# One fused attention and MLP kernel: the written order of its 1,553 jobs and 83 engine choices replaced by others

## The chip, the cores and the metric

The kernel runs on one core of a Trainium2 chip. The metric is the device time of one launch in microseconds (us). The engines are TensorE (PE in the profile, with PEld for the loading of weights), VectorE (DVE), ScalarE (ACT) and GpSimd (POOL). SyncE (SP) issues nearly all DMAs. Each engine works through a list of its own in the order in which it is written, and waits at an instruction whose input is not there yet.

## What is computed

The attention output goes into a gated MLP with a product over the sequence, and this into a second MLP with a short convolution and a sigmoid gate. Everything is float32.

```python
# attention: batch 2, 8 heads, seq 768, head_dim 64
k_sum = max of k over blocks of 32;  v_sum = mean of v over blocks of 32
scores = [band |i-j| < 16 of scale * q k^T,  scale * q k_sum^T + log(32)]
attn   = softmax(scores) @ [v, v_sum]
# first MLP: d_model 512, d_ff 1024
h = relu(x @ w_in); u, v = halves of h; v_n = layer norm of v
v_s = w_spatial @ v_n (over seq) + b_spatial
y = (u * v_s) @ w_out
# second MLP: conv over seq with 3 taps
h = relu(y @ w_in2); gate = sigmoid(conv(h)); out = (h * gate) @ w_out2
```

## The kernel before

All large products are made of three matmuls (mm3, L320 to L322): operands are split in a high part (cast, L295) and a low part (subtract, L289), and hi*hi, lo*hi and hi*lo are summed in PSUM. A product of 512 columns is three matmuls in a row, and the low part of an operand is the last that such a product waits for.

**The front** is attention, interleaved with the first product of the first MLP (x @ w_in). The 16 groups i = 0 to 15 are eight pairs of heads n, two halves g each. One group is a chain over the engines: qk on PE (L472, L479, L485), row maximum on DVE (L489), six exps on ACT (L493), their total and its reciprocal on DVE (L496, L499), the normalisation on POOL or DVE (L502), two times three transposes on PE into the PSUM tile pt (L506), each followed by a copy into SBUF on ACT or DVE (L528), and the product with the values on PE (pv, L512). Its output is copied on ACT or DVE (L533) and its low part subtracted on DVE (L534). Two score buffers (s_80 and s_81 in the lists of order below) and one pt bank are shared by all groups, so that the next qk or transpose needs the reader of the one before to be done.

Two side jobs stand in the front. The **block means** of v are made on PE from the window tile `vwin` for the pairs n = 0 and 2 (L428), and for the others on DVE with a transpose on PE (L435, L438), and are spread by L440 and L447. The **conversion of w_in** to a high and a low part takes a multiply on ACT or POOL (L304, L305), a shift (L307) and two operations on DVE that read two SBUF operands each (L309, L311), a cast and a subtract. L400, L408 and L414 prepare the windows of k and their maxima.

**The middle** is dense: the rest of the first product, the product over the sequence, the merge of w_out with w_in2 and the product with it, all mm3. **The last layer** works on halves of both operands (L716 makes sums of blocks, L295 and L289 split them, L874 mixes finished PSUM tiles into outputs) and stores the output.

**What sets the order.** A Plan collects all 1,553 jobs with what each depends on. Two tables then rule: ORDER holds the job numbers as pairs of base-64 signs, and the jobs are written to the program in this order; PICK holds, for each job that can run on more than one engine, which one is taken. So each engine's list, and the list of the DMAs that SP issues, is cut out of one order written by hand. Where the plan's own costs leave PE a gap of 0.5 us or more in the front, it writes in matmuls on `ones` (L932) that nobody reads: 17 of them in the kernel before, 6 ahead of the first qk, then 1, 8 and 2 ahead of the later ones.

Of the kernel before, what the change touches and what calls it, by code (L numbers as in the profile page):

```python
# [20 lines left out]
B, H, S, D = 2, 8, 768, 64  # L21
# [1056 lines left out]
```

## Time and profile before

| | us |
|---|---|
| median of 3 runs (330.38 to 330.89) | 330.82 |
| the profiled execution's own time | 332.48 |
| its span, first to last instruction | 330.7 |
| PE busy | 320.4 (97%) |
| DVE busy | 270.9 (82%) |
| ACT busy | 206.5 (62%) |
| POOL busy | 109.3 (33%) |

PE is the busiest by far. What it does not do in the span, about ten microseconds, lies at the start, in the first 80 us, in a short place of the last layer, and behind the last matmul. From 81 us to 284 us PE has no idle time that the table of stretches shows. The granted clock of TensorE is 1.00 in every stretch.

### The profile page before, as it was taken

The page shows a single profiled execution, that of the slowest core. Times are in us where ns is not written, and L with a number is a line of the kernel's source. Part 1 is how long each engine was busy: PE and PEld are TensorE (multiplying, and loading weights), DVE is VectorE, ACT ScalarE, POOL GpSimd, SP SyncE. Part 2 cuts the span into 40 slices and gives each one's busy share as a digit, 9 for nine tenths or more (in the row PEclk, how much of TensorE's full clock was granted, in tenths as well). Part 3 has the DMA queues.
Part 4 walks back from the last instruction along what each step waited for, and adds up shares of the span by engine and source line. Part 5 has one row for each costly group of instructions (what it writes and reads, how often), then busy time and mean ns, then how long its engine had stood idle before and what let it go on. Part 6 is the DMA issues. An engine that isn't in the chain of part 4 may idle for free.

```text
span 330.7 us, 6432 instructions
## 1 busy us (share of the span) xinstructions
PE 320.4 (97%) x2414; PEld 272.0 (82%) x2414; DVE 270.9 (82%) x501; ACT 206.5 (62%) x516; POOL 109.3 (33%) x129
## 2 busy tenths in 40 slices
PE   8887999999999999999999999999999999999995
PEld 3566878868888888888888888888888899999894
DVE  5996988997677517888969989899979999988882
ACT  3887988867456354625335545779978898955410
POOL 4686776543252146003101313020301320345510
PEclk9999999999999999999999999999999999999999
DMA  7968794842011540341333423350511330255234
GB/s 236 321 210 236 238 288 157 273 135 72 2 63 51 192 140 34 107 133 66 126 92 116 152 87 127 127 97 1 96 25 22 52 68 2 43 126 119 50 113 152
DMA packets 16640, 39.25 MB, mean 119 GB/s; under 512 B 2016, under 2 KB 8160, under 8 KB 16608
## 3 DMA queue, kind: packets, MB, share of 16 engines
q1 hardware_dynamic: 13728, 34.11, 31.6%
q0 software_dynamic: 2880, 4.72, 8.1%
q8 instruction: 19, 0.31, 0.4%
q14 instruction: 13, 0.11, 0.1%
HBM read 30.96 MB, written 3.15 MB: 103 GB/s over the span
## 4 chain that ended last, share of the span: by engine, by line
PE 85%; DVE 9%; DMA 2%; ACT 2%; issue 1%; DVEq 0%
PE late L320 11%; PE late L321 11%; PE late L322 11%; PE mm L320 8%; PE mm L321 8%; PE mm L322 8%; PE xp L321 3%; PE pt L506 3%; PE pt L321 3%; PE xp L322 3%; PE pt L320 3%; PE pt L322 3%; PE xp L320 3%; PE xp L512 3%; DMA a<-vwin 2%; DVE a L311 2%
## 5 line engine op out<-in xcount | busy, mean ns | idle before, releaser
L493 ACT ACTIVATE a<-s,a 128x120 f32<-128x120 f32 x96 | 33.2, 375 | 2.1 <-DVE a L489 2.1
L289 POOL TENSOR_TENSOR w<-a,w 128x256 fp32r<-128x256 f32 (+1 forms) x14 | 14.8, 1058 | 38.5 <-ACT w L295 38.2
L322 PE MATMUL late<-xh,a 128*128 128x512 f32 (+1 forms) x72 | 26.7, 371 | 0.0
L321 PE MATMUL late<-xl,a 128*128 128x512 f32 (+1 forms) x72 | 26.7, 371 | 0.0
L320 PE MATMUL late<-xh,a 128*128 128x512 f32 (+1 forms) x72 | 26.7, 371 | 0.0
L502 POOL TENSOR_TENSOR a<-a,a 128x720 f32<-128x720 f32 x15 | 21.3, 1422 | 9.5 <-DVE a L499 7.5
L295 ACT CAST xh<-tmp 128x384 fp32r<-128x384 f32 (+2 forms) x32 | 15.8, 510 | 9.1 <-DVE tmp L716 5.6
L752 DVE SCALAR_TENSOR_TENSOR w<-v,conv_t,w 128x1534 f32<-128x1534 f32 x10 | 18.2, 1816 | 4.0 <-ACT w L748 3.8
L493 ACT ACTIVATION_READ_ACCUMULATOR a<-s,a 128x1 f32 x96 | 21.3, 222 | 0.0
L311 DVE SCALAR_TENSOR_TENSOR a<-a,a 128x512 uint32<-128x512 uint32 (+1 forms) x24 | 18.6, 776 | 0.6
L506 PE MATMUL pt<-ident,a 128*120 128x128 f32 x96 | 16.4, 280 | 2.1 <-DVE a L528 1.8
L289 DVE TENSOR_TENSOR xl<-tmp,xh 128x384 fp32r<-128x384 f32 (+2 forms) x31 | 17.9, 586 | 0.1
L528 ACT COPY a<-pt 120x384 f32<-120x384 f32 x24 | 11.6, 482 | 9.5 <-PE pt L506 9.3
L575 DVE BATCH_NORM_STATS2 stat<-tmp 128x6 f32<-128x512 f32 x12 | 8.3, 691 | 11.2 <-ACT tmp L572 11.1
L304 ACT ACTIVATE a<-a 128x512 f32<-128x512 f32 (+1 forms) x16 | 10.1, 629 | 11.4 <-POOL w L289 4.5
L309 DVE SCALAR_TENSOR_TENSOR a<-a,a 128x512 uint32<-128x512 uint32 (+1 forms) x24 | 16.0, 665 | 1.4 <-ACT a L304 0.8
L489 DVE TENSOR_REDUCE a<-s 128x6 f32<-128x720 f32 x16 | 14.2, 890 | 3.4 <-PE s L485 3.4
L295 ACT CAST w<-a 128x512 fp32r<-128x512 f32 (+1 forms) x16 | 9.1, 566 | 12.3 <-DVE a L311 12.1
L506 PEld LDWEIGHTS pt<-ident,a 128*120 128x120 f32 x96 | 10.7, 137 | 7.0 <-DVE a L528 2.5
L320 PE MATMUL mm<-xh,a 128*128 128x512 f32 (+1 forms) x44 | 16.0, 364 | 0.0
L322 PE MATMUL mm<-xh,a 128*128 128x512 f32 (+1 forms) x44 | 16.0, 364 | 0.0
L321 PE MATMUL mm<-xl,a 128*128 128x512 f32 (+1 forms) x44 | 16.0, 364 | 0.0
(350 smaller groups left out, 1117.6 us busy)
## 6 DMA issues: line engine op xcount, KB each, us to landing
a<-w_in SPq DMA_DIRECT2D x12, 512.0 KB, 3.7
a<-w_out SPq DMA_DIRECT2D x8, 512.0 KB, 3.6
a<-vwin SPq DMA_DIRECT2D x8, 288.0 KB, 6.8
a<-v_in SPq DMA_DIRECT2D x6, 384.0 KB, 5.7
a<-vwin SPq DMA_DIRECT2D x4, 576.0 KB, 5.7
tmp<-w_spT SPq DMA_DIRECT2D x6, 384.0 KB, 3.1
a<-w_in SPq DMA_DIRECT2D x8, 256.0 KB, 6.2
a<-w_outT SPq DMA_DIRECT2D x4, 512.0 KB, 3.7
```

Source lines behind the costliest of these rows:

```text
L289: eng.tensor_tensor(out=lo.r(), in0=src.f(), in1=hi.f(), op=ALU.subtract)
L295: us = {"ACT": (0.2 + n / 1200, lambda: ACT.copy(hi.r(), src.f())), "POOL": (0.12 + n / 1050, lambda: POOL.tensor_copy(hi.r(), src.f()))}
L309: add({"DVE": (0.16 + n / 960, lambda: DVE.scalar_tensor_tensor(out=last.u(), in0=fu.u(), scalar=0x80000000, in1=last.u(), op0=ALU.bitwise ...
L311: add({"DVE": (0.16 + n / 960, lambda: DVE.scalar_tensor_tensor(out=fu.u(), in0=fu.u(), scalar=3, in1=last.u(), op0=ALU.logical_shift_left ...
L320: PE.matmul(ps, lhsT=lh, rhs=rh, start=first and i == 0, stop=False, **kinds)
L321: PE.matmul(ps, lhsT=lh, rhs=rl, start=False, stop=False, **kinds)
L322: PE.matmul(ps, lhsT=ll, rhs=rh, start=False, stop=last and i == n - 1, **kinds)
L489: DVE.tensor_reduce(out=st[:, 0], in_=sv, op=ALU.max, axis=AX.X, negate=True)
L493: ACT.activation(out=e[:, u, :NK], in_=sv[:, u // GA, u % GA], func=AF.Exp, bias=st[:, 0, u:u + 1], accum_out=sm[:, u, :1])
L502: eng.tensor_tensor(out=e, in0=e, in1=st[:, 1].unsqueeze(2).to_broadcast([128, GB, NK]), op=ALU.mult)
L506: PE.transpose(pt3[:NK, a], e[:, GA * h + a, :NK], ident)
L752: DVE.scalar_tensor_tensor(out=two(ct)[:, bs, to], in0=two(h)[:, bs, of], scalar=scale(k), in1=two(ct)[:, bs, to], op0=ALU.mult, op1=ALU.add)
```

## The change

Nothing but the two tables is replaced. The same jobs are written in another order, and some run on another engine. The first 481 places of the new ORDER hold the attention front and the first part of the first product; the later jobs stand in another order as well. Of the choices in PICK 83 differ. Over the program POOL has 12 rows fewer and DVE 2 more. In the part up to the small conversion of the convolution's weights (L974) DVE has three L528 copies more, one L502, one L400 and one L414 more, two L447 and one L440 less. The matmuls on `ones` go from 17 to 15: 6 ahead of the first qk, 5 ahead of the second, 4 ahead of the transposes of group 2.

```diff
--- before.py
+++ after.py
 ORDER = (
-    "ABASACAFAEAUAGAiATADAHAjAgAkAAAhALAqAVAWAIAMBKBYAXArAYA3BaAZAsANAJBbBZBL
...
+    "AAACABADAFAgAEAiAGAjAZAaAkAhAbAHAqAcAdAeArALBYAfAMBZBbBaBcAIA3A4AsAJAlAt
...
 )
 PICK = (
...
-    "111111010100101001011100110000000010000101001100010010000001110000001200
...
+    "001101210000101011001110100010000010100011000100011010100010111010000100
...
```

**First place, DVE.** This is DVE's list around the row maximum of group 2 (L489 on s_80) in the kernel before, up to the first copy of transposes (L528). a_0_124 and a_0_195 are the buffers in which w_in is converted.

```order
L489 TENSOR_REDUCE a_0_90<-s_80 128x6
L496 TENSOR_REDUCE a_0_95<-a_0_95 128x6
L499 RECIPROCAL a_0_95<-a_0_95 128x6
L309 SCALAR_TENSOR_TENSOR a_0_97<-a_0_124,a_0_97 128x256
L311 SCALAR_TENSOR_TENSOR a_0_195<-a_0_195,a_0_97 128x256
L408 TENSOR_REDUCE a_0_90<-a_0_91 128x12
L528 COPY a_0_92<-pt 120x384
```

The same place after the change, where a_0_156 is the buffer of the conversion:

```order
L307 TENSOR_SCALAR a_0_97<-a_0_156 128x256
L309 SCALAR_TENSOR_TENSOR a_0_97<-a_0_156,a_0_97 128x256
L311 SCALAR_TENSOR_TENSOR a_0_156<-a_0_156,a_0_97 128x256
L499 RECIPROCAL a_0_90<-a_0_90 128x6
L489 TENSOR_REDUCE a_0_90<-s_80 128x6
L496 TENSOR_REDUCE a_0_95<-a_0_95 128x6
L499 RECIPROCAL a_0_95<-a_0_95 128x6
L408 TENSOR_REDUCE a_0_90<-a_0_91 128x12 x2
L528 COPY a_0_92<-pt 120x384
```

The conversion in the second buffer (a_0_195) has left this place. One conversion, L307, L309 and L311 of 256 columns, stands ahead of the row maximum, and between the row maximum and the copy L528 stand only two short operations and the two L408.

**Second place, PE.** This is PE's list around the block means of pair n = 2 (mm_85 is the PSUM tile of the means, L428). Before, the first half stands behind the transposes of group 5, with the scores of group 7 behind it:

```order
L485 MATMUL s_80<-a_0_95,a_0_231 64x120 x12
L438 MATMUL xp<-ident,a_0_86 24x128
L506 MATMUL pt<-ident,a_0_100 120x128 x3
L428 MATMUL mm_85<-a_0_233,a_0_86 24x128 x6
L472 LDWEIGHTS ones
L472 MATMUL s_81<-a_0_86,ones 64x3x24
```

After the change:

```order
L485 MATMUL s_81<-a_0_95,a_0_252 64x120 x12
L512 MATMUL xp<-a_0_92,a_0_492 64x64 x12
L506 MATMUL pt<-ident,a_0_91 120x128 x3
L428 MATMUL mm_85<-a_0_236,a_0_86 24x128 x12
L506 MATMUL pt<-ident,a_0_91 120x128 x3
L512 MATMUL xp<-a_0_92,a_0_492 64x64 x12
```

Both halves of the means now stand together, behind the scores of group 7, a product L512 of group 4 and the first transposes of group 6; ahead of that there is also one product of the first MLP of 256 columns.

**Third place, DVE in the last layer.** Before, between the mixes L874 of the second output half, w_1_2380 being the last of two, and the next mix:

```order
L874 TENSOR_TENSOR w_1_2380<-mm_85,w_1_2380 128x384
L716 TENSOR_TENSOR a_2_2617<-tmp_0_1227,w_1_2533 128x384
L289 TENSOR_TENSOR xl_0_102<-tmp_0_1227,xh_0_101 128x384
L716 TENSOR_TENSOR tmp_0_1227<-tmp_0_1227,w_1_2696 128x384
L289 TENSOR_TENSOR xl_0_102<-a_2_2617,xh_0_101 128x384
L716 TENSOR_TENSOR tmp_0_1227<-tmp_0_1227,w_1_2607 128x384
L289 TENSOR_TENSOR xl_0_104<-tmp_0_1227,xh_0_103 128x384
L289 TENSOR_TENSOR xl_0_102<-tmp_0_1227,xh_0_101 128x384
L874 TENSOR_TENSOR w_1_2533<-w_1_2533,late_1299 128x384
```

After the change:

```order
L874 TENSOR_TENSOR w_1_2412<-mm_85,w_1_2412 128x384
L716 TENSOR_TENSOR a_2_2663<-tmp_0_1208,w_1_2526 128x384
L289 TENSOR_TENSOR xl_0_102<-tmp_0_1208,xh_0_101 128x384
L716 TENSOR_TENSOR tmp_0_1208<-tmp_0_1208,w_1_2572 128x384
L289 TENSOR_TENSOR xl_0_102<-a_2_2663,xh_0_101 128x384
L289 TENSOR_TENSOR xl_0_102<-tmp_0_1208,xh_0_101 128x384
L874 TENSOR_TENSOR w_1_2464<-pt,v_2_2846 128x384
```

Two operations fewer stand between the mixes and the last subtract into xl: one sum L716 and one subtract L289 are elsewhere. POOL's list has three L289 in a row here, into xl_0_102, xl_0_104 and xl_0_99, where before it had an L289 into xl_0_104, a sum L716 and an L289 into xl_0_99.

## Rows read from the trace of the kernel before

**Rows 1.** the page: time of each engine, then shares of the chain that ended last

```profile
PE 320.4 (97%) x2414; PEld 272.0 (82%) x2414; DVE 270.9 (82%) x501; ACT 206.5 (62%) x516; POOL 109.3 (33%) x129
...
PE 85%; DVE 9%; DMA 2%; ACT 2%; issue 1%; DVEq 0%
```

**Rows 2.** busy us by stretch (x matmuls or operations), PEclk, DMA share, GB/s

```profile
0.00:21.00 21.00, 18.24 (x240) 10.72 (x242) 16.17 (x50) 13.73 (x56) 13.11 (x27) 1.00 0.81 261
21.00:41.00 20.00, 18.00 (x351) 13.99 (x346) 16.71 (x38) 16.97 (x79) 14.27 (x19) 1.00 0.80 232
41.00:61.00 20.00, 19.71 (x261) 16.63 (x264) 17.37 (x37) 17.79 (x63) 12.42 (x16) 1.00 0.74 234
61.00:81.00 20.00, 19.28 (x246) 15.64 (x236) 18.59 (x31) 13.74 (x55) 9.35 (x9) 1.00 0.45 139
...
284.00:315.00 31.00, 30.56 (x176) 29.89 (x175) 27.09 (x53) 18.86 (x46) 15.89 (x17) 1.00 0.39 84
```

**Rows 3.** waits view of PE: line, awaited engine, tile and line: us, times, longest

```profile
PE mm L428 <- DMA a<-vwin: 1.9, 2, 1.7
PE pt L506 <- DVE a L528: 1.8, 2, 1.2
PE mm L932 <- DVE mhalf L926: 1.0, 1, 1.0
PE xp L321 <- DVE xl L289: 0.4, 1, 0.4
```

**Rows 4.** timeline of DVE, 11 to 17 us: start us, us, line, tiles

```profile
11.66 1.54 DVE L309 SCALAR_TENSOR_TENSOR a<-a,a 128x256 uint32<-128x256 uint32 x1
...
14.23 0.38 DVE L309 SCALAR_TENSOR_TENSOR a<-a,a 128x256 uint32<-128x256 uint32 x1
14.53 1.61 DVE L311 SCALAR_TENSOR_TENSOR a<-a,a 128x256 uint32<-128x256 uint32 x1
```

**Rows 5.** timeline of POOL in the same stretch

```profile
14.46 1.40 POOL L502 TENSOR_TENSOR a<-a,a 128x720 f32<-128x720 f32 x1 [1.54 <-DVE a L499]
```

**Rows 6.** timeline of PE, 12 to 22 us; in brackets idle time before it

```profile
12.57 1.49 PE L428 MATMUL mm<-a,a 96*24 96x128 f32 x12 [0.16 <-DMA a<-vwin]
...
17.12 0.54 PE L506 MATMUL pt<-ident,a 128*120 128x128 f32 x3 [1.16 <-DVE a L528]
...
21.53 0.52 PE L506 MATMUL pt<-ident,a 128*120 128x128 f32 x3 [0.27 <-POOL a L414]
```

**Rows 7.** timeline of SP's issue and of PE's means, 21 to 28 us

```profile
21.29 2.84 SPq L386 DMA_DIRECT2D a<-vwin  x3
...
27.92 0.94 PE L428 MATMUL mm<-a,a 96*24 96x128 f32 x7 [1.73 <-DMA a<-vwin]
```

**Rows 8.** timeline of POOL, DVE and PE, 67 to 71 us

```profile
67.56 1.83 POOL L502 TENSOR_TENSOR a<-a,a 128x720 f32<-128x720 f32 x1
...
68.18 1.77 DVE L311 SCALAR_TENSOR_TENSOR a<-a,a 128x512 uint32<-128x512 uint32 x1
...
70.47 0.54 PE L506 MATMUL pt<-ident,a 128*120 128x128 f32 x3 [0.61 <-DVE a L528]
```

**Rows 9.** groups by line on DVE, 5 to 105 us: count, busy us, mean ns

```profile
L528 DVE COPY a<-pt 120x384 f32<-120x384 f32 x8 | 4.4, 548 | 1.6 <-PE pt L506 1.6
...
L447 DVE TENSOR_SCALAR a<-a 24x768 f32<-24x768 f32 x2 | 1.2, 615 | 0.2 <-ACT a L440 0.2
...
L502 DVE TENSOR_TENSOR a<-a,a 128x720 f32<-128x720 f32 x1 | 0.9, 899 | 0.0
```

**Rows 10.** timeline of POOL, DVE and PE in the last layer, 308 to 314 us

```profile
310.30 1.33 POOL L289 TENSOR_TENSOR xl<-tmp,xh 128x384 fp32r<-128x384 f32 x1
...
308.91 0.55 DVE L289 TENSOR_TENSOR xl<-tmp,xh 128x384 fp32r<-128x384 f32 x1
309.38 1.38 DVE L716 TENSOR_TENSOR tmp<-tmp,w 128x384 f32<-128x384 f32 x1
...
313.85 0.45 PE L321 MATMUL xp<-xl,a 128*128 128x384 f32 x1 [0.44 <-DVE xl L289]
```

More of the change, by code (lines that the diff above doesn't have):

```diff
@@ new lines @@
+    "CuClCmCnEfCKC3CvCwCaDhDMBPDWBQFNE0DiCxEpCyCzDXC0DYEqErDsCBDxDNDODPBWDjFMDZDaDAC5DtDQFOFPDkDlC6DbDcE1E2DmDnCCDyEUFVDdDoEs"
+    "EtDpEuC7C8C9C+C-BXEiDqDBCLFiEvFjE3E4EjEkDzD0EwFvCMCNDuDvCOCPD6DCDDDED7D8D9D1D+D2EEEFD3FBCQEGE5EmDFDGFkEHEIE6D4F6F7EOEPEQ"
+    "ERGmD5F8F9C4FCD-EAEBECFWEXE7FFFGEYEZEaEbGnFHFIFJFKElFXEDE8GlEcEdE9FYFLGkFZFlFaGQGRGDE+ExEJEKELESHRGSGEGFEyFmE-FAFnEzFbFz"
+    "F0EMFwGtG6GdEVJ8FQFRFcFdF1ENHHHIGeF2F3GfGGGgF4FeHSFSFTF5FoHJFUHTGhGiGjFpFqFrGuFDG7HUHVHKHLEWFsG8GTGUGHF+GVGIFtHMHNFuFfFg"
@@ new lines @@
+    "HlHmFxHnHoGJFyG9G+HOHWHbHcGvGKGwHdHXFhHpHYItGLGMF-GxGyGAHZH5GBHqIDH6HeGWGXIyGCH7FEGoH8HPHfHgGYHrHvGNGZGaGbHwHxHaGOGcGPHh"
+    "G-J5GzJ6GpG0HQH9H+HyGqLNIEG1G2GsGrH-IFIuHAHzH0HBIzINIOIPHCIIIvHsIAHiH1H2HtHuHDH3H4IBICIXIiI0HEG3IJIKHFLOLPHGILISI1G4G5Hj"
+    "I2HkITInIdIaIUIQIYIZIMLQIjIqIVIWIkIlIGIRIoIpI6LRIHIbIcI3JHJIJJImIrIeJbLbI9I+JKIwJvI7IsJ7LUI8IfIxIgI4I5JLJMJNJwI-JAJBJCKH"
+    "JDIhJcJRKbKIJSJxKcKdJTJlJEJUJdJOKJLWJmJyJVKRJ9JnKlKeJFJ+J-KKKLJeKMKSJWKmJGJzKAKfJPJ0JQJfJXJoJ1LDJ2J3KvKwJYJZJpK5KBJgLSJ4"
@@ new lines @@
+    "JaKNJhKCJiJqK6JjJrKOLELFK7LTLGLVMrJsKDKxLXMsMhKPJtLYKELZKnKgKFKTJkLaLdLcMiKUJuLiLeLfKhLgLpKoKiKpLhKjMjLkKyK8KqKGKVM-LjKW"
+    "KzLlK9MkLmLrLnKkLwKrMlLoLqK0NAMtKXKsMmKQLsLtM1KYK1LuK+MnK-LvLHLxM2MuKtK2LyLzK3L3KZL0LANTL1K4L+L2M3MvNJM4MoKaLIL4NdL5MwNK"
+    "M5MpL6L7KuLJL8L9MxM6NeNBL-M7NCMFMyMAMBMCNUMDMzNfMqLKMEM0NDNLNnNVLBNgOvNhMGNiNoM8LLMHOpMMNMMINEOqMTNWNXMJLCNYM9MKNZO1NFML"
+    "OrNjO2MOO3NkMNMPMQNpO4MVOsNqOwMaNNMRLMNOMSNrOxMUNlNxM+OtNsPHNaMWMXO7MYNGOuO8OyMZO9NPNtPTNmNQO5MbMcN4MdOzMeNRNHNyMfPUPVNz"
@@ L78 @@
+    "TrVyTuWdTbUAV7VrWhVzTtVPWBVsWnWwWVUHTkVtV0VUXVWxWeVVV1UBVSWiTnV2VuV3ToXdWyXZWpVXVQVvWfVwXeUIWqWoWLW0TpTvVWXaWzWFXfWMWNW7"
+    "W1TwWjXGXbWsVxW3VYWrUQWuWkW8WGW2WHWOXHWIWvV8WCW9XcWPWtXIXTXRWJW+WQW4XJXgW5XCW-X-X5V4XDXmXhXNUCXnXiXOW6XoXjXpXKXkXqXlXAXM"
+    "XBV9XEWKYAXLXyXzXrX0X6WDXPXFT8XsXQX1XtXSX7V+WEXUYBXXX2XWX3XuXvYCX8XwX4XxYLXYYDYFYGYMX9YNYEYOYHYPYIX+YJYQYK"
 )
 PICK = (
[L80 removed]
@@ L84 @@
+    "011000000000000100000000000000000000000000000000000000000000000000000000000000000000000000100010000000000000100000001000"
+    "0000001001000100000000001010100"
 )
```

43 lines of the change are left out of this document (13 added, 30 removed).

## The prediction

> **What bounds the kernel now.** The first view to read is the page's time by engine and its chain: PE is busy for 320.4 us of the 330.7 us of the span, and 85% of the chain that ended last is PE [rows 1]. Both tables of the change only move work that already exists, so the question is where PE stands still, and the table of busy time by stretch tells that [rows 2]. PE stands idle for 21.00 - 18.24 = 2.76 us in the first 21 us, 2.00 us from 21 to 41, 0.29 us from 41 to 61, 0.72 us from 61 to 81, and 0.44 us from 284 to 315. The stretches between have none. These five make 6.21 us; the rest lies behind the last matmul, where mixes and stores follow that no order of the earlier jobs shortens. The waits view names what PE waits for [rows 3]: 1.9 us on DMAs of vwin ahead of the block means, 1.8 us on DVE's copies out of pt, 1.0 us at the very start on a constant, which every order has, and 0.4 us on a subtract in the last layer. So at most 6.21 - 1.0 = 5.2 us of idle time can be won, the 1.0 being that of the start.
>
> Two timelines show why DVE is late. In the first, L309 and L311 of 256 columns, which read two SBUF operands, take 1.54 and 1.61 us, where the same L309 takes 0.38 us a moment later [rows 4]. POOL's L502 runs from 14.46 to 15.86 in the same time [rows 5], and L311 ends 0.3 us behind it. The copy L528 stands behind L311 on DVE, and so PE's transposes at 17.12 come after 1.16 us of waiting [rows 6]. At 68 us the pattern repeats: POOL's L502 from 67.56 to 69.39, L311 stretched to 1.77 us, and PE waits 0.61 us [rows 8]. In the last layer a sum L716 takes 1.38 us beside POOL's L289, where a subtract of the same size takes 0.55 us, and PE waits 0.44 us [rows 10].
>
> **The change part by part.** I take five terms: three stretches of the front, the last layer, and what the new order may cost unseen.
>
> A, the first 21 us. The new order has the same attention work on PE up to the transposes of group 2, and the same nine matmuls on `ones` behind the first qk (5 and 4 in place of 1 and 8). What goes is the wait of 1.16 us: the second conversion leaves its place ahead of the copy, and what is left between the row maximum and the copy are reductions. The 0.27 us at 21.53 [rows 6] goes too. Of the idle 2.76 us, 1.0 stays, so 1.7 us can be won at most, and nothing if new waits come for old. New waits are likely here: the first block means now stand ahead of the third qk, and their vwin, though issued some places earlier, is among the first DMAs; before, the means waited 0.16 us for it at 12.57 [rows 6]. The DMA engines are at 0.81 of their time [rows 2], so some other load pays for each that is moved up. I take half of the gain, -0.9 us, with -1.7 and 0 as bounds.
>
> B, 21 to 41 us. The largest single wait of PE is here: vwin of pair 2 is issued at 21.29, and the means start at 27.92 after 1.73 us [rows 7]. Now the first half of the means stands behind a product of 256 columns, the scores of group 7, a product L512 and transposes of group 6. The transposes alone take 0.54 us [rows 6]; I estimate the four jobs at four times that, some 2 us, which is more than the wait. And the issue itself, which waits for the product L512 of group 0 to release the buffer, comes as much earlier as PE gains in A. So the first half should find its data. The second half now follows at once, while its vwin can be issued only when the product of group 1 has released its half of the buffer; it takes part of the wait over. I take half, -0.9 us of the 2.00 idle, with -1.8 and 0 as bounds.
>
> C, 41 to 105 us. The idle time is 0.29 + 0.72 = 1.01 us. Its main row, 0.61 us at 70.47 [rows 8], goes with a collision that the new lists avoid as far as they show it: the L502 of POOL that met the conversion of 512 columns stands among reductions and copies of DVE. I take -1.0 us; 0 is the other bound.
>
> D, the last layer. Between the mixes and the last subtract DVE has five operations in place of seven. Each is worth 0.47 us, the step from one start at 308.91 to the next at 309.38 [rows 10], so DVE reaches the subtract that PE awaits about 0.9 us earlier, and the 0.44 us can go: -0.4 us. POOL's three L289 in a row of 1.33 us each [rows 10] are on the other side. Each can hold a DVE operation for 1.38 - 0.55 = 0.83 us, and two more such meetings than before would cost up to 1.7 us. Bounds -0.4 and +1.7.
>
> E, what an order does not show. The three meetings of [rows 4, 8, 10] cost PE 1.16 + 0.61 + 0.44 = 2.2 us. An order does not say which of two operations starts first, and others will meet; so I charge a fifth of that, +0.4 us, bounds 0 and +1.5.
>
> Of these meetings the rows show that an operation of DVE with two SBUF operands takes 1.54 us where it takes 0.38 us by itself [rows 4]. The Trainium skill ("SBUF — State Buffer", section "Who interferes with whom") states that DVE's second read port is shared with GpSimd, that the first to start holds it for its whole operation, and that DVE operations with at most one SBUF input outside its two-port modes do not contend. By that rule an order that lays reductions beside POOL's operations pays nothing, E would be 0 and the sum -3.2 us, 327.6 us; the trace agrees in so far as the stretched rows all have two SBUF operands, and the rule speaks against the last layer, below.
>
> The work itself is nearly level: of L528, L502 and L447, DVE gets 3 x 0.55 + 0.90 - 2 x 0.615 = 1.3 us more [rows 9], hidden as long as DVE has gaps: 40 - 17.37 - 18.59 = 4.0 us from 41 to 81 [rows 2].
>
> The sum is -0.9 - 0.9 - 1.0 - 0.4 + 0.4 = **-2.8 us**. The profiled execution took 332.48 us, 1.8 us more than its span of 330.7, so a profile of the changed kernel should show a span near 327.9. The median of 330.82 is 1.66 us under that execution; I subtract the same 2.8 us from it, which gives 328.0 us.
>
> **The rivals.** *DVE becomes the bound (slower).* Place: 41 to 81 us, where DVE has 4.0 us of gaps [rows 2]. It gets 1.3 us more from the three groups above, and if four of its two-operand operations there meet POOL that do not now, at 1.38 - 0.55 = 0.83 us each [rows 10], 3.3 us more: 4.6 us. It decides from the point at which the gaps cannot take that in; row maxima must follow their scores at once, so I count half of the gaps as usable, and 2.6 us are left over. Then C does not come, and A and B come half: 330.8 + 2.6 - 0.9 = 332.5 us. For it speaks the density, DVE being busy for 18.59 of 20 us from 61 to 81; against it, that the new list has fewer conversions directly ahead of copies.
>
> *The front is bound by loads.* DMA engines are busy 0.81 and 0.80 of the first 41 us [rows 2], and each wait on a copy is only followed by one on q or vwin. Then A and B give 0.2 us together, C and E stay: 330.8 - 0.2 - 1.0 - 0.4 + 0.4 = 329.6 us. The two waits on vwin [rows 3] speak for it; against it, that SP and not the DMA engines held the vwin of pair 2.
>
> *The last layer gives it back.* POOL's L289 in a row hold the subtracts: D is +1.7 us, and A and B come half, C at -0.8, E at 0 since it is priced here: 330.8 - 0.9 - 0.8 + 1.7 = 330.8 us, within 0.2% of now. It decides from two meetings more than now. For it speaks that the three L289 stand in a row; against it, that POOL's L289 and L716 stood in alternation before and met DVE as well [rows 10]. By the rule of the Trainium skill (the same section) the first to start keeps the port, so DVE would lose the rest of POOL's 1.33 us each time that it comes second; the 1.38 us of [rows 10] agrees.
>
> *The front waits go whole.* A -1.7, B -1.5, C -1.0, D -0.4, E +0.4: 326.6 us. For it, the loads that SP holds back come earlier by all that PE gains.
>
> **How the numbers follow.** The forecast has 0.53: 328.0 us, from 327.2 to 329.0. Whole gain 0.13, loads 0.13, last layer 0.10, DVE 0.11. The range that should hold the time 8 times in 10 runs from 326.2 (A -1.5, B -1.7, C -1.0, D -0.4) to 330.8, which leaves out most of the slower rival and a little at the low end. Two runs of this kernel can be told apart from about 0.2% on, 0.66 us: faster than 330.16 is 0.53 + 0.13 + 0.13 = 0.79, within it 0.10, slower 0.11.
>
> **What would show it right or wrong.** In the waits view of the changed kernel the longest wait on L528 should be under 0.5 us, and that on vwin under 1.0 us. The transposes of group 2 should come near 20.7 us in place of 21.53. L309 and L311 should take under 1 us in most rows up to 75 us. In the last layer PE should have less than 0.44 us idle. The prediction is wrong if the busy table shows 2 us or more idle for PE in both of the first two stretches, or idle time from 61 to 105 us that DVE ends, or new idle time between 105 and 284 us, where the later jobs are in another order too and PE has none now.

## The result and the profile after

The changed kernel took **326.86 us** (median of 8 runs, 326.34 to 332.24), the kernel before beside it 330.54 us (median of 8, 329.79 to 330.94). The ratio is **0.9895**, with a 95% interval from 0.9871 to 0.9919: about 3.5 us faster. The forecast was 328.0 us, a gain of 2.8 us, in a range from 326.2 to 330.8; the direction was right and the time lies in the range, just below the band from 327.2 to 329.0 that the forecast itself was given. The sum came near for reasons that are only partly those of the working, and partly by luck, as the runs below show.

The first profiled execution of the changed kernel took 332.24 us and holds a disturbance that most executions do not have (it has its own section at the end), so the lines here are those of a second profile of the same kernel, which took 327.1 us for a span of 325.2 us. Against [rows 1], the time of each engine, then the shares of the chain that ended last:

```profile
PE 318.3 (98%) x2412; PEld 272.2 (84%) x2412; DVE 266.9 (82%) x508; ACT 206.8 (64%) x516; POOL 99.5 (31%) x122
...
PE 90%; DVE 3%; DMA 2%; POOL 2%; SPq 1%; issue 1%; POOLq 0%
```

Against [rows 2], the same stretches: width, then busy us of PE, PEld, DVE, ACT, POOL (with counts), PEclk, DMA share, GB/s:

```profile
0.00:21.00 21.00, 18.90 (x257) 11.24 (x261) 15.78 (x53) 15.05 (x69) 12.41 (x25) 1.00 0.88 268
21.00:41.00 20.00, 19.28 (x355) 15.56 (x349) 17.30 (x41) 17.80 (x71) 15.79 (x20) 1.00 0.87 246
41.00:61.00 20.00, 20.00 (x310) 17.50 (x304) 17.95 (x37) 17.87 (x66) 10.52 (x15) 1.00 0.76 239
61.00:81.00 20.00, 20.00 (x193) 16.30 (x194) 16.20 (x37) 15.59 (x59) 7.43 (x8) 1.00 0.54 149
...
284.00:315.00 31.00, 30.65 (x177) 30.23 (x176) 26.55 (x48) 14.49 (x34) 14.80 (x16) 1.00 0.42 103
```

PE stands idle for 2.10 us, 0.72 us, nothing, nothing, and 0.35 us, where [rows 2] had 2.76, 2.00, 0.29, 0.72 and 0.44. What is left is named by the waits view of PE (awaited engine, tile and line: us, times, longest), against [rows 3]:

```profile
PE mm L932 <- DVE mhalf L926: 1.0, 1, 1.0
PE pt L506 <- DVE a L528: 0.6, 1, 0.6
PE mm L428 <- DMA a<-vwin: 0.4, 1, 0.4
PE pt L320 <- DVE v L874: 0.3, 1, 0.3
PE s L485 <- DMA a<-q_in: 0.3, 1, 0.3
```

**A second profile of before** changes what these are to be compared with. It took 329.62 us for a span of 327.9 us, 2.8 us less span than the execution that the prediction was read from. Its stretches and waits:

```profile
0.00:21.00 21.00, 18.35 (x242) 10.74 (x242) 16.60 (x51) 14.12 (x58) 13.56 (x28) 1.00 0.86 265
21.00:41.00 20.00, 19.46 (x352) 15.19 (x353) 19.16 (x40) 18.05 (x80) 14.65 (x19) 1.00 0.85 250
41.00:61.00 20.00, 19.73 (x303) 16.85 (x301) 17.67 (x37) 17.15 (x59) 12.88 (x15) 1.00 0.78 242
61.00:81.00 20.00, 20.00 (x202) 16.46 (x199) 17.65 (x36) 14.86 (x62) 8.30 (x9) 1.00 0.39 125
```

```profile
PE pt L506 <- DVE a L528: 1.1, 1, 1.1
...
PE mm L428 <- DMA a<-vwin: 0.5, 1, 0.5
PE xp L321 <- DVE xl L289: 0.4, 1, 0.4
PE xp L512 <- DVE xl L534: 0.4, 1, 0.4
PE pt L506 <- POOL a L414: 0.3, 1, 0.3
```

The wait on the copy is there again, with 1.1 us. The 1.73 us on vwin [rows 7] and the 0.61 us at 70 us [rows 8] are not: PE's idle time from 21 to 41 us is 0.54 us and not 2.00, from 61 to 81 us nothing and not 0.72. The experiments below give more profiles of these places in the old order. The wait on the copy is in all five that keep it: 1.16, 1.05, 0.91, 1.38 and 1.83 us. The 1.73 us on vwin, on which term B rests, is in one of four that keep the means in their place, the first. The 0.61 us, the main row of term C, comes again in one of five more, with 0.48 us (see conv_later). So the wait on vwin was, as far as four profiles tell, an accident of one execution, and the other comes and goes. This second profile is not a usual execution either: its span of 327.9 us is the shortest of the eight of that run, whose median is 328.8 us.

**Where the gain lies**, worked out from the start times of the same matmuls in the two second profiles: up to the transposes of group 2 the new order is 0.92 us earlier (20.27 in place of 21.19), up to the 300th matmul of the dense products (L320 to L322, counted by their starts) 2.39 us (116.34 in place of 118.73), up to the last matmul 2.25 us (321.15 in place of 323.40). From the 300th dense matmul on PE needs 204.81 us in place of 204.67. So of PE's gain the attention front brings everything, and the new order of the later jobs nothing. Another 0.37 us lies behind the last matmul: from its start to the end of the span it is 4.45 us before and 4.08 us after. The working had held that stretch to be fixed.

### The profile page after: what moved, and what is told of

Its sections match the earlier page's. It is cut to its first block, busy times and chain, and to the rows that moved or that the text cites. A ratio compares the mean times of both kernels' runs of the same rounds, so it can differ in the third digit from the quotient of the medians.

```text
span 330.4 us, 6408 instructions
## 1 busy us (share of the span) xinstructions
PE 320.4 (97%) x2412; PEld 273.7 (83%) x2412; DVE 267.1 (81%) x508; ACT 206.6 (63%) x516; POOL 99.4 (30%) x122
## 4 chain that ended last, share of the span: by engine, by line
PE 90%; DVE 4%; DMA 2%; issue 1%; SPq 1%; POOL 1%; POOLq 0%
PE late L321 11%; PE late L320 11%; PE late L322 11%; PE mm L320 10%; PE mm L321 9%; PE mm L322 9%; PE pt L506 3%; PE pt L320 3%; PE pt L322 3%; PE pt L321 3%; PE xp L321 3%; PE xp L320 3%; PE xp L512 3%; PE xp L322 3%; PE s L485 3%; DMA a<-vwin 2%
## 5 line engine op out<-in xcount | busy, mean ns | idle before, releaser
L320 PE MATMUL late<-xh,a 128*128 128x512 f32 (+1 forms) x72 | 26.7, 371 | 0.0
L322 PE MATMUL late<-xh,a 128*128 128x512 f32 (+1 forms) x72 | 26.7, 371 | 0.0
L289 POOL TENSOR_TENSOR w<-a,w 128x256 fp32r<-128x256 f32 (+1 forms) x14 | 14.1, 1010 | 37.1 <-ACT w L295 36.9
L580 POOL TENSOR_TENSOR stat<-stat,mhalf 128x1 f32<-128x1 f32 x12 | 7.8, 655 | 51.3 <-DVE stat L577 47.5
L289 DVE TENSOR_TENSOR a<-tmp,a 128x256 fp32r<-128x256 f32 (+2 forms) x28 | 18.3, 673 | 5.4 <-ACT a L295 5.4
L502 POOL TENSOR_TENSOR a<-a,a 128x720 f32<-128x720 f32 x14 | 19.7, 1415 | 7.0 <-DVE a L499 6.7
L714 POOL DMA_DIRECT2D tmp<-w x9 | 7.9, 951 | 36.0 <-ACT tmp L713 24.4
L295 ACT CAST w<-a 128x512 fp32r<-128x512 f32 (+1 forms) x15 | 8.2, 548 | 16.9 <-DVE a L311 16.8
L304 ACT ACTIVATE a<-a 128x512 f32<-128x512 f32 (+1 forms) x20 | 12.4, 622 | 9.4 <-POOL w L289 5.1
L528 ACT COPY a<-pt 120x384 f32<-120x384 f32 x21 | 10.3, 489 | 12.8 <-PE pt L506 12.7
L295 ACT CAST a<-tmp 128x256 fp32r<-128x256 f32 (+2 forms) x26 | 14.2, 549 | 5.5 <-DVE tmp L716 4.0
L289 DVE TENSOR_TENSOR xl<-tmp,xh 128x384 fp32r<-128x384 f32 (+2 forms) x29 | 17.4, 604 | 0.1
L485 PE MATMUL s<-a,a 64*64 64x120 f32 x384 | 13.6, 265 | 3.3 <-issue 2.6
L322 PE MATMUL mm<-xh,a 128*128 128x512 f32 (+1 forms) x44 | 16.0, 364 | 0.0
```

The source lines that it names most:

```text
L289: eng.tensor_tensor(out=lo.r(), in0=src.f(), in1=hi.f(), op=ALU.subtract)
L295: us = {"ACT": (0.2 + n / 1200, lambda: ACT.copy(hi.r(), src.f())), "POOL": (0.12 + n / 1050, lambda: POOL.tensor_copy(hi.r(), src.f()))}
L304: mul = {"ACT": (0.2 + n / 1080, lambda: ACT.mul(fu.f(), half(1).bitcast(F32), 2.0 ** -112)), "POOL": (0.18 + n / 1050, lambda: POOL.tenso ...
L320: PE.matmul(ps, lhsT=lh, rhs=rh, start=first and i == 0, stop=False, **kinds)
L322: PE.matmul(ps, lhsT=ll, rhs=rh, start=False, stop=last and i == n - 1, **kinds)
L485: PE.matmul(sv[c * QB:(c + 1) * QB, h, a], lhsT=qts[j].ap[rows, blk * QB:(blk + 1) * QB], rhs=kws[j].ap[rows, blk * NK:(blk + 1) * NK], st ...
```

## The experiments

**The changed kernel again** (`after_again`), without an edit, for a second profile.

> The changed kernel once more, for a profile of an execution like its usual ones. Its first profile holds a stall of 2.29 us inside a qk of group 13 at 67.7 us, in which PE waited for nothing that the profile shows, and then 3.7 us of matmuls at half the granted clock; its span of 330.4 us is 5 us above that of most of its executions. If that stall is an accident of one execution, the time is 326.5 to 327.2 us, the span about 325, and PE has under 0.5 us idle from 61 to 81 us. If the new order causes it as a rule, the wait on nothing at the qk returns and the span is 327 or more.

Measured: 327.0 us median of 7 (325.93 to 329.8), ratio 0.9902 [0.9868, 0.9937]. The result stands; its profile is the one shown above.

**The new front with the old rest** (`front_new`), and **the old front with the new rest** (`later_new`). In the first, the first 481 places and the choices of their jobs are the changed kernel's, and the remaining jobs follow in the sequence and with the choices of before; the second is its mirror. The table of front_new against that of the changed kernel, from the place at which they part:

```diff
-    "G-J5GzJ6GpG0HQH9H+HyGqLNIEG1G2GsGrH-IFIuHAHzH0HBIzINIOIPHCIIIvHsIAHiH1H
...
+    "G-J5J6IiIEGzHyGpG0GqGsLNHzHQHiH9G1G2H+IFIIGrHAINIOHBHjHCH0HsG3HDH1HkHEI
...
```

> The first 481 places are those of the changed kernel with their engines; all other jobs in the order and on the engines of the kernel before. Theory of the prediction (the front's waits make the gain, terms A, B and C; the last layer some 0.4 us): 3.0 to 3.3 us under the kernel before, about 327.4 us, with PE idle 0.44 us in the last layer as before. Rival, that the later order makes most of it: under 1.5 us gain, 329 us or more. If the join of the two orders costs something, PE shows idle time between 100 and 130 us.

> The first 481 places of the kernel before with their engines; all other jobs in the order and on the engines of the changed kernel. Theory of the prediction: the waits of the front stay (1.2 us on a copy at 17 us, 1.7 us on vwin at 26 us), the last layer gains 0.4 us: 0.2 to 0.7 us under the kernel before, 329.9 to 330.4 us. Rival, that the later order makes most of the gain: 2 us or more under it.

Measured: front_new 329.29 us, ratio 0.995 [0.9932, 0.9968]; later_new 331.01 us, ratio 1.0017 [0.9998, 1.0037]. The new rest on the old front gives no gain. The new front with the old rest gives about half of it by the ratio, a third by the medians. That misses the 3.0 to 3.3 us expected, and its time is the one expected of the rival by which the later order makes the gain; but later_new shows that it doesn't. The profile of front_new shows where the other half stays. The waits view of PE, and the stretch from 81 to 105 us:

```profile
PE mm L320 <- ACT tmp L572: 1.3, 1, 1.3
```

```profile
81.00:105.00 24.00, 22.69 (x203) 18.86 (x202) 16.25 (x34) 11.74 (x23) 6.75 (x7) 1.00 0.13 39
```

Up to 86 us PE is as early as in the changed kernel's second profile: the transposes of group 2 start at 20.28 (20.27 there), and all later transposes up to there within 0.02 us of the same time or 0.25 us earlier. So the gain of the front is there. It is lost behind the join: PE waits 1.3 us for ACT at 94 us, and the 300th dense matmul starts at 118.38, only 0.35 us earlier than in the second profile of before. That the old rest waits there because it was laid out for another front is a reading and has no run of its own. So the front and what directly follows it are one piece, and a cut at place 481 measures the seam too.

**One job moved** (`conv_later`): the kernel before, with one part of the conversion in the second buffer behind the first copy. It is the part of term A that the working spoke of, by itself. DVE's list, where a1_0_195 is that buffer:

```diff
 L309 SCALAR_TENSOR_TENSOR a11_0_97<-a0_0_124,a11_0_97 128x256
+L408 TENSOR_REDUCE a4_0_90<-a8_0_91 128x12
+L528 COPY a10_0_92<-pt_82 120x384
 L311 SCALAR_TENSOR_TENSOR a1_0_195<-a1_0_195,a11_0_97 128x256
-L408 TENSOR_REDUCE a4_0_90<-a8_0_91 128x12
-L528 COPY a10_0_92<-pt_82 120x384
```

> The kernel before with one job moved: the operation L311 of 256 columns on the second conversion buffer, which ran beside POOL's L502 at 14.5 us, goes behind DVE's first copy L528. Term A alone. If the meeting causes PE's wait of 1.16 us on that copy, the wait is under 0.3 us; if waits in the front add up, the time falls by 0.8 to 1.2 us. If loads or PE's own instruction blocks come at their own time, the transposes of group 2 come earlier but the time falls by less than 0.4 us. If L502 is not the cause, the copy's wait stays over 0.8 us.

Measured: 329.14 us median of 12, ratio 0.9958 [0.9938, 0.9978], 1.4 us faster with one job of 1,553 moved, somewhat more than the 0.8 to 1.2 us expected; the wait on the copy is gone, as expected. DVE's timeline (start, us, line):

```profile
13.61 0.39 DVE L309 SCALAR_TENSOR_TENSOR a<-a,a 128x256 uint32<-128x256 uint32 x1
14.37 0.55 DVE L528 COPY a<-pt 120x384 f32<-120x384 f32 x1
14.84 0.69 DVE L311 SCALAR_TENSOR_TENSOR a<-a,a 128x256 uint32<-128x256 uint32 x1
```

The copy runs at 14.37 and not at 16.19, L311 takes 0.69 us and not 1.61, and the transposes of group 2 start at 19.65, 1.54 us earlier than in the second profile of before. Against that profile the lead stays at 1.46 us up to 66 us. Then 0.97 us of it is lost at one place, the place of [rows 8], and the 300th dense matmul is at 118.24, 0.49 us earlier. POOL's, DVE's and PE's timelines of conv_later there:

```profile
64.24 1.83 POOL L502 TENSOR_TENSOR a<-a,a 128x720 f32<-128x720 f32 x1
...
64.86 1.76 DVE L311 SCALAR_TENSOR_TENSOR a<-a,a 128x512 uint32<-128x512 uint32 x1
...
67.14 0.55 PE L506 MATMUL pt<-ident,a 128*120 128x128 f32 x3 [0.48 <-DVE a L528]
```

This is the meeting of [rows 8] over again, at the same jobs: L311 takes 1.76 us beside POOL's L502, where it takes 0.69 us in the second profile of before, and PE waits for the copy behind it. The profiled execution of conv_later is a usual one (329.10 us, median 329.14). If usual executions of the kernel before have this loss too, their span is 1.0 us longer than the 327.9 us of the second profile, which agrees with their median of 328.8 us; no profile of such an execution was taken, so that is a reading. It would explain why the medians keep the whole 1.4 us, which is the measured worth of the first conversion's place.

**The means moved** (`mean_later`): the kernel before, with the first half of the means of pair 2 moved directly ahead of the second half. It is term B by itself. PE's list:

```diff
 L506 MATMUL pt<-ident,a_0_100 120x128 x3
-L428 MATMUL mm_85<-a_0_233,a_0_86 24x128 x6
+L932 MATMUL mm_84<-ones 128x512   (five of these, put in by the plan's rule for gaps)
 L472 MATMUL s_81<-a_0_86,ones 64x3x24
...
-L428 MATMUL mm_85<-a_0_233,a_0_86 24x128 x6
+L428 MATMUL mm_85<-a_0_233,a_0_86 24x128 x12
```

> The kernel before with one job moved: the first half of the block means of pair 2 (L428) goes directly ahead of the second half, behind the scores of group 7, two transposes and a product. Term B alone. If waits in the front add up to the end, the 1.73 us on vwin go or shrink to under 0.5 us, and the time falls by 0.9 to 1.5 us. If loads bound the front, PE meets the same time again at the second half of the means or at the next load, and the time falls by less than 0.3 us.

Measured: 332.36 us, ratio 1.0047 [1.0022, 1.0072]: slower, which neither side of the expectation had. Its profile also has a stop of 1.64 us inside a product at 49.61, which looked like the price, so a further kernel took that away (`mean_light`): the same, with two v loads moved behind the k load of pair 7. SP's list:

```diff
 L303 DMA a_0_124<-w_in 128x512
+L303 DMA a_0_195<-w_in 128x512
+L373 DMA a_0_96<-k_in 128x800
 L382 DMA a_0_151<-v_in 128x768
-L303 DMA a_0_195<-w_in 128x512
 L382 DMA a_0_231<-v_in 128x768
-L373 DMA a_0_96<-k_in 128x800
```

> The kernel with the first half of the block means of pair 2 moved later (1.64 us of PE standing still at 49.6 us, waiting for no data), and now two loads moved as well: v of pairs 4 and 5 (384 KB each) are issued behind the load of k of pair 7 instead of at 40.7 and 41.6 us. Theory of instruction blocks: PE stands still at 49.6 us because the block of its own instructions (a packet of 16 KB of kind instruction, at 47.1 to 48.1 us) lies in the DMA queues behind those loads; with 768 KB less ahead of it the packet comes 1 us or more earlier, the stall shrinks to under 0.6 us, and the time falls by 0.8 us or more against that kernel's 332.4. Rival, that the stall is a wait on DVE's L489 as the waits view puts it: the stall stays, 332 to 333 us, and late v adds a wait of DVE.

Measured: 331.49 us, ratio 1.0045 [1.0025, 1.0066]. The stop at 49 us is gone from the profile, and by its ratio the kernel is as much slower than before as mean_later is (the medians differ by 0.9 us). So the stop is not the price of the move. That price is read from PE's timeline, first in the second profile of before, then in mean_light:

```profile
25.80 1.49 PE L428 MATMUL mm<-a,a 96*24 96x128 f32 x12
27.21 0.23 PE L472 MATMUL s<-a,ones 64*64 64x72 bf16 x4
...
29.43 1.49 PE L428 MATMUL mm<-a,a 96*24 96x128 f32 x12
```

```profile
25.94 1.24 PE L932 MATMUL mm<-ones 128*128 128x512 bf16 x5
27.36 0.23 PE L472 MATMUL s<-a,ones 64*64 64x72 bf16 x4 [0.18 <-ACT a L493]
...
29.58 2.80 PE L428 MATMUL mm<-a,a 96*24 96x128 f32 x24
```

The scores of group 7 (L472) cannot start before ACT has done its exps, and come at 27.21 and 27.36 alike. Ahead of them the first half of the means filled PE's gap; with the means gone, five matmuls on `ones` and a wait of 0.18 us stand there, 1.42 us by the starts, and the means cost their 1.3 us later. Of these 1.3 us 0.4 us comes back at 38 us, where a wait of 0.35 us on L534 is gone; the ratio of mean_light makes 1.5 us. The changed kernel has a product of 256 columns there, which is work that has to be done anyway, and a wait of 0.61 us on a copy just ahead of it.

**The two tables apart**: the order of before with the changed choices (`picks_only`), and the changed order with the choices of before (`order_only`).

```diff
 # picks_only: PICK of the changed kernel in the kernel before
-    "111111010100101001011100110000000010000101001100010010000001110000001200
+    "001101210000101011001110100010000010100011000100011010100010111010000100
 # order_only: PICK of the kernel before in the changed kernel
-    "001101210000101011001110100010000010100011000100011010100010111010000100
+    "111111010100101001011100110000000010000101001100010010000001110000001200
```

> The order of the kernel before with the 83 engine choices of the changed one. If engines alone bring a good part of the gain (POOL's operations out of DVE's way): 1 us or more under the kernel before. If the choices only fit the order with which they were made: no gain or slower, 330.3 to 333 us, with new waits of PE on DVE from 40 to 100 us.

> The order of the changed kernel with the engine choices of the kernel before. If the order alone brings the gain: 326.8 to 328 us. If order and choices are needed together: 329 us or more, with waits of PE on DVE's or POOL's operations that the changed kernel does not have.

Measured: picks_only 340.38 us, ratio 1.0307 [1.0272, 1.0341]; order_only 346.76 us, ratio 1.0484 [1.0452, 1.0515]. Each half of the change alone costs about three and five times what both together gain, and picks_only lies far above the 330.3 to 333 us expected of it. The longest waits of PE in picks_only:

```profile
PE pt L506 <- ACT a L528: 2.4, 4, 1.2
PE mm L320 <- ACT v L595: 1.9, 2, 1.7
```

and in order_only:

```profile
PE s L472 <- ACT a L493: 5.0, 2, 3.4
PE pt L506 <- ACT a L528: 2.0, 3, 1.0
```

The waits are mostly on copies and exps; the reading is that an engine has got another engine's work at a place where the order leaves no room for it. In order_only the granted clock also falls, to 0.91 from 41 to 61 us and 0.83 from 61 to 81 us, in the stretches in which PE stands still for 1.84 us (up to 48.95) and 3.45 us (up to 70.71). In picks_only it stays at 1.00, with PE busy for only 15.11 us from 41 to 61 us. The plan also writes in 17 more matmuls on `ones` in picks_only (41 with those of the preamble, against 24), so the waits listed are not all of PE's empty time.

**Without matmuls on `ones`** (`after_nofill`): the changed kernel without the 15 in its gaps.

```diff
-                if self.fill and gap >= 0.5:
+                if self.fill and gap >= 50.0:
```

> The changed kernel without the 9 matmuls on ones that stand behind the first qk and ahead of the transposes of group 2 and the 6 ahead of the first qk, which nobody reads. The change took two of them away, and PE's time in them went from 8.0 to 7.5 us. If they only fill time in which PE waits anyway, the time stays within 0.5 us of the changed kernel, 326.4 to 327.4 us, and the granted clock stays at its upper level. If they keep the clock up, matmuls of the front run at the lower level for some us and the time is 328 us or more. If they delay the work behind them, it is under 326.3 us.

Measured: 329.69 us, ratio 0.9981 [0.9959, 1.0004], some 2.7 us slower than with them. The waits of PE and the first stretch:

```profile
PE s L485 <- DMA a<-q_in: 3.8, 2, 2.3
```

```profile
0.00:21.00 21.00, 15.97 (x227) 10.69 (x227) 13.96 (x49) 13.30 (x58) 10.53 (x23) 0.84 0.83 245
```

The gaps that they fill are waits for q, which stay, with 2.25 and 1.59 us at the first two rows of L485. In this execution the clock is lost too: PEclk is 0.84 in the first 21 us where it is 1.00 with them. It is at the lower level from 7.7 to 14.5 us, and the first half of the means takes 2.75 us in place of 1.49. The transposes of group 2 come at 22.13 in place of 20.27. That the clock makes the whole 2.7 us is not shown: this execution with 328.83 us is one of the faster of the twelve, and its mean clock of 0.987 is the lowest of all. Whether two fewer of these matmuls, as in the change, gain anything by themselves no run shows.

**Other places for two loads** (`after_light`, and once more as `after_light_again`): the changed kernel, with the load of b_sp 60 places ahead of its first use, and the v load of pair 6 behind a vwin load. SP's list:

```diff
 L382 DMA a_0_252<-v_in 128x768
-L1020 DMA sp_0_1152<-b_sp 128x768
+L386 DMA a_0_492<-vwin 96x1536
 L382 DMA a_0_162<-v_in 128x768
-L386 DMA a_0_492<-vwin 96x1536
...
 L303 DMA a_1_1519<-w_outT 128x1024
+L1020 DMA sp_0_1792<-b_sp 128x768
```

> The changed kernel with two loads moved: b_sp (384 KB, used at about 125 us) leaves the group of six loads issued from 55 to 60 us and is issued 60 places ahead of its first use, and v of pair 6 is issued behind vwin of pair 5. Theory of instruction blocks: the packet with PE's instructions at 63 to 68 us has 384 KB less ahead of it, comes 1 us or more earlier, and the executions of 328 us and more (4 of 15 so far) become rare; the median is 326.3 to 326.9 us. Rival, that those executions come from elsewhere: 3 or more of 12 stay at 328 us or more, the median at 326.9.

> The kernel of after_light once more, in more rounds: the changed kernel with the load of b_sp 60 places ahead of its first use and the load of v of pair 6 behind vwin of pair 5, and nothing left out. The question is whether the executions of 328 us and more, 4 of 15 in the changed kernel and 0 of 6 in after_light, come from PE's own instruction block standing behind data loads. If so, none or at most one of some ten executions is at 328 or above, the median stays at 327.0 to 327.3, and in the profile the instruction packet near 64 us ends there and PE has no stop of 1 us or more behind it. If those executions have another cause, about a quarter of them, 2 to 3 of ten, are at 328 to 332 again.

Measured: 327.17 us median of 6 (326.97 to 327.43), ratio 0.991 [0.9893, 0.9927], and 326.7 us median of 4 (326.08 to 327.02), ratio 0.9888 [0.9866, 0.9911]. The medians are near that of the changed kernel, and both lie outside what was expected, one above and one below. Of 15 executions of the changed kernel 4 took 328 us or more, of these 10 none. If the true share were 4 of 15, ten in a row without one would come about once in 22 times ((11/15) to the tenth is 0.045). But that share is itself known from 15 executions only: that four long ones among 25 all fall among the first 15 comes once in nine times (0.108). So the difference is not settled.

**The kernel before again** (`before_again`), for the second profile shown above.

> The kernel before once more, for a second profile. Its first profile shows a time of 332.48 us where most of its executions take 329.4 to 330.9, and holds 1.73 us of waiting on vwin at 27.9 us, with 15 of 16 parts of that load there by 25.2 us and the last at 27.9. If that wait is an accident of the one execution, it is under 0.5 us here, the span is 328 to 329 us, and the gain of the change in usual executions has no such term B. If it is the rule, it is 1.5 us or more again.

Measured: 330.58 us median of 8 (329.62 to 330.98), ratio 1.0 [0.9984, 1.0017].

## Why the prediction held, step by step

**A, the first 21 us: right, in mechanism and in size.** Forecast -0.9 us, measured -0.92 us at the transposes of group 2. The other profiles bear it out: with the old front these transposes start at 20.99 to 21.53 us (four profiles) and at 22.88 in later_new, whose PEclk is 0.92 in that stretch; with the new one and its matmuls on `ones` they start at 20.10 to 20.49 (five). By the steps of PE from start to start, the means with the wait behind them go from 3.96 to 2.84 us, which is the wait on the copy, and the product ahead of the wait on L414 from 1.19 to 0.85. Against that the steps of L479, behind which the qk L485 now waits for q, rise from 1.03 to 1.52 us. That some other load pays for each one moved up was what half the gain was charged for. conv_later shows that the first conversion's place alone is worth it. PE's timeline in the second profile of before, then in the changed kernel: the transposes behind the first copy start without a wait.

```profile
16.79 0.54 PE L506 MATMUL pt<-ident,a 128*120 128x128 f32 x3 [1.05 <-DVE a L528]
...
21.19 0.51 PE L506 MATMUL pt<-ident,a 128*120 128x128 f32 x3 [0.27 <-POOL a L414]
```

```profile
15.80 0.54 PE L506 MATMUL pt<-ident,a 128*120 128x128 f32 x3
...
20.27 0.55 PE L506 MATMUL pt<-ident,a 128*120 128x128 f32 x3
```

**E and the collisions: better than forecast.** I charged 0.4 us for new meetings of DVE and POOL. There are none among the conversions: against [rows 4], DVE's timeline of the changed kernel, and its groups from 5 to 105 us (count, busy us, mean ns):

```profile
11.46 0.42 DVE L309 SCALAR_TENSOR_TENSOR a<-a,a 128x256 uint32<-128x256 uint32 x1 [0.18 <-ACT a L304]
11.92 0.42 DVE L311 SCALAR_TENSOR_TENSOR a<-a,a 128x256 uint32<-128x256 uint32 x1
```

```profile
L311 DVE SCALAR_TENSOR_TENSOR a<-a,a 128x256 uint32<-128x256 uint32 x8 | 3.4, 425 | 0.3
L309 DVE SCALAR_TENSOR_TENSOR a<-a,a 128x256 uint32<-128x256 uint32 x8 | 3.4, 422 | 0.7 <-POOL a L305 0.3 <-ACT a L304 0.2
```

The same groups in the second profile of before:

```profile
L311 DVE SCALAR_TENSOR_TENSOR a<-a,a 128x256 uint32<-128x256 uint32 x8 | 6.1, 764 | 0.1
L309 DVE SCALAR_TENSOR_TENSOR a<-a,a 128x256 uint32<-128x256 uint32 x8 | 5.1, 636 | 0.9 <-ACT a L304 0.8
```

Sixteen operations of the same size take 6.8 us in place of 11.2 us. Before, six rows of L309 and L311 of 256 and 512 columns up to 75 us took 0.90 to 1.65 us where others took 0.38 to 0.84; after, none takes over 0.70 us. This is the clearest difference between the two kernels. All six profiles with the front of before, its choices included, have six or seven rows of 0.89 us or more, and of the five with the new front and its matmuls on `ones` four have none and after_light_again one, with 0.93 us. What the new front lays beside POOL's operations are reductions and copies: in conv_later a reduction L408 (13.91 to 14.46) and the copy L528 (14.37 to 14.92) run inside POOL's L502 (13.84 to 15.24) and take their usual 0.55 us. The rule that I gave beside the sum, in the Trainium skill's "SBUF — State Buffer", section "Who interferes with whom", fits these rows. It would have had E at 0 and 327.6 us, 0.4 us nearer to what was measured.

**B, 21 to 41 us: wrong.** The step that failed is the wait of 1.73 us [rows 7], taken as the kernel's own. In the second profile the vwin loads cost PE 0.5 us in all, at another place (12.34 us), and conv_later and later_new, which keep the means where they were, have no wait at them either. mean_later and mean_light, which make this move alone, are slower, because the means had a gap of PE to fill that the working did not look for. From 21 to 41 us the idle time of PE is 0.72 us after the change and 0.54 us before.

**C, 41 to 105 us: the mechanism holds, the size is open.** Forecast -1.0 us. The meeting of [rows 8] belongs to the old order: conv_later has it again, where it costs about 1.0 us, and in mean_later, mean_light and later_new the L309 ahead of that L311 is the stretched one (1.50, 1.15 and 1.74 us), without a wait of PE that the list shows. The second profile of before has no such cost, so in the pair of profiles the term has no main row. In that pair PE gains 97.54 - 96.07 = 1.47 us between the transposes of group 2 and the 300th dense matmul, for the stretches of B and C together, against 1.9 us forecast. By the steps of PE it is spread: 0.84 us in the steps of dense matmuls, 0.57 us in those of transposes, 0.51 us for the two matmuls on `ones` that are no longer there (they were in no term of the sum), 0.2 us in means and products L512, less 0.67 us in the small transposes L438, where the one wait of 0.6 us on a copy now stands. No single wait carries it. If usual executions of the kernel before have the meeting, as that of conv_later has, its 1.0 us comes on top.

**D, the last layer: wrong in effect.** The 0.44 us on the subtract [rows 10] is gone, as forecast. But another wait has come, in PE's timeline of the last layer:

```profile
296.73 0.45 PE L320 MATMUL pt<-v,a 128*128 128x384 f32 x1 [0.35 <-DVE v L874]
```

later_new has it too. From the 300th dense matmul to the last PE needs 0.14 us more than before. The working also read [rows 10] too narrowly. POOL's operation that the sum at 309.38 met was first of all an L716 (309.13 to 310.33), which those rows leave out. And the steps of DVE behind that sum were not 0.47 us but 1.28 to 1.30 us, since the next two operations were stretched as well (1.37 and 1.36 us). The rival by which POOL's three L289 in a row give 1.7 us back did not come either: they follow each other in POOL's list, but the second and the third wait for a cast of ACT (1.09 and 1.46 us), and the three start 2.5 us apart (301.94, 304.45 and 306.92).

**The rivals.** DVE as the bound did not come: DVE is busy 16.20 us from 61 to 81 us, against 17.65 in the second profile of before, though over the program it has 7 operations more and POOL 7 fewer (508 and 122 in the page, 501 and 129 before; the description of the change gives other counts). Loads as the bound came in a small part, as the wait for q. The rival of whole front waits named 326.6 us, which is nearer to the measured 326.86 than the forecast, but not by its terms: it had A at -1.7 us and B at -1.5, and A came with -0.92 and B's wait was not there to be won.

**The sum** was -2.8 us for some -3.5 us measured. By the pair of profiles A was right, C and B together too large by 0.4 us, D by 0.5 us, the charge E by 0.4 us the other way, and the end behind the last matmul, in no term, gave 0.37 us; the span falls by 327.9 - 325.2 = 2.7 us. The spans of usual executions fall by more, from a median of 328.8 us (before_again) to 325.0 us. The 1 us between lies in the executions of before that are longer than the profiled one; the meeting of [rows 8] has that size in conv_later, but no trace of such an execution shows it. So the nearness of the sum is in part luck: B counted 0.9 us for a wait that usual executions don't have, and the two matmuls on `ones` and the end of the program made up for it. The forecast of a span near 327.9 us for the changed kernel failed by 2.7 us, for the same reason as B: it subtracted a gain from an execution that was itself 2.8 us too long. That the median was forecast from the median kept the error out of the time.

**The signs that were named**: the transposes near 20.7 us (20.27), the wait on vwin under 1.0 us (0.4), L309 and L311 under 1 us, and no new idle time from 105 to 284 us hold. The longest wait on L528 was to be under 0.5 us and is 0.6; less than 0.44 us of idle time in the last layer holds with 0.35, at another place.

## What to carry to other kernels

Before a wait is put into a sum, look for it in further profiles of the same kernel: of the waits of the kernel before, the copy's 1.16 us, the 0.27 on L414 and the 0.44 in the last layer came back in the second within 0.12 us, and the two others, 1.73 and 0.61, were gone. One further profile does not settle it either: the 0.61 us came back in a third, and the second was the fastest of its eight executions. When a job is moved off its place, ask what it was filling there: the half of the means that waited for its load was at the same time PE's cover for ACT's exps. An order written by hand and the choices of engines in it are one object: here each alone made the kernel 3 to 5% slower, and together they make it 1% faster.

## What the runs showed of the hardware that was not expected

**PE stops for its own instructions.** The page lists, among the DMA queues, one of kind "instruction" (packets, MB, share of 16 engines):

```profile
q8 instruction: 19, 0.31, 0.4%
```

That is 19 packets of 16 KB, about one for every 256 of PE's 4,824 matmuls and weight loads. In the first profile of the changed kernel (332.24 us) one of them is late. A window of the DMA view, 67.2 to 67.3 us, has the packet's start in it:

```profile
q8 instruction: 1, 0.02, 81.7%
```

0.817 x 16 x 0.1 us makes 1.31 us, so it ends near 68.6 us. PE's timeline in the same profile:

```profile
66.95 0.78 PE L485 MATMUL s<-a,a 64*64 64x120 f32 x19
70.02 0.43 PE L485 MATMUL s<-a,a 64*64 64x120 f32 x5 [2.29 <-issue]
...
71.63 0.63 PE L321 MATMUL mm<-w,xh 128*128 128x512 f32 x1
```

In the middle of a row of 24 matmuls with all their operands there, PE stands still for 2.29 us and goes on 1.4 us behind the end of the packet. In the second profile the same packet starts at 63.6 and PE runs through the same row without a stop. Two smaller stops in the first profile, 0.30 us at 33.71 and 0.19 us at 26.39, also end about 1.5 us behind such a packet, and so does the 1.64 us of mean_later, with its packet from 47.1 to 48.1:

```profile
49.61 0.40 PE L321 MATMUL mm<-xl,w 128*128 128x512 f32 x1 [1.64 <-DVE a L489]
```

The view puts this one down to DVE's row maximum, which is no input of this matmul. In mean_light, with other loads ahead, the packet starts at 45.3 and there is no gap; in the second profile of before, with no load moved, it starts at 45.4. That these stops belong to the packets fits their places too: counted by start among PE's matmuls and weight loads, they stand behind 705, 962 and 1,986 of them in the first profile and behind 1,473 in mean_later, which is 257, 1,024 and 511 apart from the one at 962, each a multiple of 256 within one. What makes a packet late stays open. Loads in front of it in the DMA queues are a guess that these runs don't bear out: the vwin load of 576 KB issued around 58 us took 10.7 us to land in the first profile and 10.2 us in the second. In both profiles of the kernel with its two loads moved the packet starts between 63 and 64 us and PE has no such stop, but so it does in the second profile of the changed kernel.

The Trainium skill ("Runtime: NRT & Kernel Launch", section "Instruction fetch mechanics") states that a sequencer fetches its instructions in blocks of 16 KiB, 256 instructions, by a DMA queue of its own and that the cost of crossing a block is mostly hidden. The size and the 256 agree with the packets and places here, and mostly hidden too: in the first profile of the changed kernel three of the 19 cost anything, in the second none. The stop of 2.29 us is the exception that the word leaves open.

**What the stop costs beyond itself.** Behind it the granted clock falls: matmuls of 512 columns take 0.63 us in place of 0.40 us up to 73.7 us. The stretch in the first profile of the changed kernel:

```profile
61.00:81.00 20.00, 17.70 (x205) 14.39 (x202) 12.19 (x25) 13.41 (x50) 8.00 (x8) 0.91 0.39 106
```

That an execution of 328 us and more has this cause each time is not shown: only the profiled ones have a trace. Of the four long ones two list a mean clock of 0.994 and 0.995, and two 0.999 and 1.0, so at most two can hold such a fall of the clock.
